# The order of routing work around the scores, in gated linear attention followed by a mixture of experts

## The chip, the cores and the metric

The kernel runs on one core of one Trainium2 chip. The metric is the device time of one launch in microseconds (us). A core has five engines, each with its own stream of instructions that it works through in order: TensorE (PE in the profile), VectorE (DVE), ScalarE (ACT), GpSimd (POOL) and SyncE (SP, which here issues transfers). An engine waits for another by semaphores. The kernel is scheduled by hand: on each engine, instructions stand in the order in which the program issues them, so moving a call in the program moves its instructions in their engines' streams.

## What is computed

Attention first: a recurrence over 768 steps for each of 4 x 8 heads of width 48. Its outputs, as 3072 rows of 384, go through a top-1 mixture of 8 experts.

```python
def _attn_ref(q, k, v, alpha):
    state = zeros(B, H, D, D)
    for t in range(S):                       # B, H, S, D = 4, 8, 768, 48
        state = alpha[:, :, t, :, None] * state + einsum('bhd,bhe->bhde', k[:, :, t], v[:, :, t])
        y[:, :, t] = einsum('bhd,bhde->bhe', q[:, :, t], state)

def _moe_ref(x, w_gate, w1, w2):             # x: 3072 x 384; E = 8; F = 1024
    logits = x @ w_gate
    expert_idx = argmax(logits, axis=1)
    probs = exp(logits - logits.max(-1)); probs /= probs.sum(-1) + 1e-9
    gate_w = probs[arange(N), expert_idx]
    # rows sorted by expert (stable), then for each expert e:
    #     y = relu(x_e @ w1[e]) @ w2[e],  put back in the rows' order
    return gate_w[:, None] * y
```

## The kernel before

The 3072 rows are 24 blocks of 128 (`NT` = 24), and the blocks go through a software pipeline two at a time ("a pair", s and s + 1). Block s is made in steps that lie in different pairs: `logs` and `cums` (decays), `operands` (k and q multiplied with decays, on GpSimd), `transposes`, `scores` (k with q, masked), `products` (k with v), `state`, `reads` and `weighs` (the output), `rows` (output as rows, and logits).

```python
def operands(s, k=nc.gpsimd, q=nc.gpsimd):       # L364, L366
    kq = kqb[s % 4]
    k.tensor_tensor(kq[:, 0, :, :D], d["k"][:], heads(d["icp"]), op=ALU.mult)
    q.tensor_tensor(kq[:, 1, :, :D], d["q"][:], d["cp"], op=ALU.mult)

def scores(s):                                   # L386 to L393
    sA = ps.tile([C, NP, C], F32, name="sA")     # one PSUM bank each
    sB = ps.tile([C, NP, C], F32, name="sB")
    ...                                          # products of kT and qT into sA and sB
    nc.vector.tensor_tensor(d["dA"][:], sA[:], cmask[...], op=ALU.mult)
    nc.scalar.copy(d["dB"][:], sB[:])
    nc.gpsimd.affine_select(d["dB"][:], d["dB"][:], ...)

def products(s):                                 # L452 to L460: into the same banks sA (s odd) or sB (s even)
    ...
    if s % 2:
        nc.vector.tensor_tensor(d["acc"][:], kv, st[s - 1]["U"][:, :, :D], op=ALU.add)   # accA
    else:
        nc.scalar.copy(d["acc"][:], kv)                                                  # accB

def rows(s):                                     # L478, L480
    ...                                          # products into xr
    nc.vector.reduce_sum(lgn[:, s, :], xr[...], axis=AX)       # logits, negated
```

The routing goes on beside attention. Four blocks are a group (the last two groups have two). When the logits of a group are there, `choose` finds each row's expert on VectorE and adds up on GpSimd how many rows before it have chosen each expert; later `rank_products` and `slots_of` make each row's slot of it, and `one_hots` prepares, for one block, what turns slots into lists of rows.

```python
def choose(g):                                   # g: the blocks of a group; L496 to L504
    nc.vector.tensor_reduce(lmin[:, t], lgn[:, t, :], axis=AX, op=ALU.min)
    nc.vector.tensor_tensor(sc[:], lgn[:, t, :], lmin[...], op=ALU.is_le)
    nc.vector.tensor_tensor(sc[:], sc[:], first_w[...], op=ALU.mult)
    nc.vector.reduce_max(top[:], sc[:], axis=AX)
    nc.vector.tensor_tensor(oh[:, t, :], sc[:], top[...], op=ALU.is_equal)
    for s in g:
        nc.gpsimd.tensor_add(ohs[:, s + 1, :], ohs[:, s, :], oh[:, s, :])

def one_hots(s, eng=nc.vector):                  # L579, L580
    nc.vector.tensor_scalar(oh_r[:, s, :], iota_r[:], scalar1=rc[:, 0, :], scalar2=None, op0=ALU.is_equal)
    eng.tensor_scalar(oh_c[:, s, :], iota_h[:], scalar1=rc[:, 1, :], scalar2=tokv[...], op0=ALU.is_equal, op1=ALU.mult)
```

The loop over pairs, cut to its order:

```python
for s in range(2, NT - 2, 2):
    ...
    reads(s); reads(s + 1)
    weighs(s, 0); weighs(s, 1)
    products(s + 1); products(s + 2)
    weighs(s + 1, 0); results_to(s, y, 0)        # yT, on VectorE
    weighs(s + 1, 1); results_to(s, y, 1)
    state(s + 1)
    if hots: one_hots(hots.pop(0))
    scores(s + 2)
    do(cums, s + 5)
    ranked = [rank_products(g, ...) for g in groups_of if g[-1] == s - 1]
    ...
    transposes(s + 3); do(operands, s + 5); state(s + 2)
    rows(s); keep_rows(s)
    do(cums, s + 6); do(transposes, s + 4)
    rows(s + 1); keep_rows(s + 1)
    scores(s + 3)
    do(operands, s + 6)
    store_rows(s)
    late_consts(s + 2); late_consts(s + 3)       # small constants, on GpSimd
    if s == ORD: choose(groups_of[-2])           # ORD = 20
    if hots: one_hots(hots.pop(0))
    for g in groups_of[:-2]:
        if g[-1] == s + 1: choose(g)             # s = 2, 6, 10, 14, 18
```

Behind the loop the last two blocks are finished, the lists of rows are made, and rows are gathered by them (`xg`). Meanwhile TensorE works ahead on expert 0's first layer, for the two blocks (EB = 2) of rows that were gathered early: 24 products of 128 x 128 by 128 x 256, `go_ahead(n)` issuing n of them. Then blocks 2 and 3 are turned (transposed by TensorE into `xtp`, copied by VectorE into `xT`) and the first layer goes on with their columns:

```python
go_ahead(9)
for k in range(EB, needed[0][-1] + 1):           # k = 2, 3
    turn_block(k)
    go_ahead(3)
go_ahead(99)
layer1(w_t[0][0], xT[0], h_t[0], EC, cols[0])
```

Of the kernel before, what the change touches and what calls it, by code (L numbers as in the profile page):

```python
# [18 lines left out]
def kernel(  # L19
# [70 lines left out]
    groups_of = [range(a, b) for a, b in zip(ends, ends[1:])]  # L90
    ORD = NT - 4
# [197 lines left out]
    with tc.tile_pool(name="ld", bufs=6) as ld, \  # L289
# [90 lines left out]
        def scores(s):  # L380
            d = st[s]
            sA = ps.tile([C, NP, C], F32, name="sA")
            sB = ps.tile([C, NP, C], F32, name="sB")
            for p in range(NP):
                for t, r in ((sA, 0), (sB, DP)):
                    nc.tensor.matmul(  # L386
                        t[:, p, :], lhsT=d["kT"][r : r + D, p, :], rhs=d["qT"][r : r + D, p, :], start=True, stop=True,
                    )
            d["dA"] = work.tile([C, NP, C], F32, name="dA")
            nc.vector.tensor_tensor(d["dA"][:], sA[:], cmask[:, None, :].to_broadcast([C, NP, C]), op=ALU.mult)  # L390
            d["dB"] = work.tile([C, NP, C], F32, name="dB")
            nc.scalar.copy(d["dB"][:], sB[:])  # L392
            nc.gpsimd.affine_select(  # L393
                d["dB"][:], d["dB"][:], compare_op=ALU.is_ge, fill=0.0,
                base=0, pattern=[[0, NP], [1, C]], channel_multiplier=-1,
            )
# [92 lines left out]
        def store_rows(s):  # L489
            r0 = s * C + (s >= NT // 2)  # L490
            nc.sync.dma_start(x_d[r0 : r0 + C, :], st[s]["xs"][:])

        def choose(g):

            t, n = slice(g[0], g[-1] + 1), len(g)
            nc.vector.tensor_reduce(lmin[:, t], lgn[:, t, :], axis=AX, op=ALU.min)  # L496
            sc = work.tile([C, n, E], F32, name="sc")
            nc.vector.tensor_tensor(sc[:], lgn[:, t, :], lmin[:, t].unsqueeze(2).to_broadcast([C, n, E]), op=ALU.is_le)
            nc.vector.tensor_tensor(sc[:], sc[:], first_w[:, None, :].to_broadcast([C, n, E]), op=ALU.mult)
            top = work.tile([C, n], F32, name="top")  # L500
            nc.vector.reduce_max(top[:], sc[:], axis=AX)
            nc.vector.tensor_tensor(oh[:, t, :], sc[:], top[:].unsqueeze(2).to_broadcast([C, n, E]), op=ALU.is_equal)
            for s in g:
                nc.gpsimd.tensor_add(ohs[:, s + 1, :], ohs[:, s, :], oh[:, s, :])  # L504

# [25 lines left out]
        def close_early(pos):  # L531

            cnt = work.tile([1, 1], F32, name="cnt")
            nc.vector.tensor_scalar(cnt[:], pos, scalar1=float(EC), scalar2=-1.0, op0=ALU.min, op1=ALU.mult)
            nc.vector.scalar_tensor_tensor(
                ohs[0:1, TE, 0:1], in0=cnt[:], scalar=float(EC), in1=ohs[0:1, TE, 0:1], op0=ALU.add, op1=ALU.add,
            )
# [47 lines left out]
        def tokens_of_slots(t0, t1):  # L585
            for t in range(t0, t1):
                nc.tensor.matmul(
                    route[:, :NC], lhsT=oh_r[:, t, :C], rhs=oh_c[:, t, :NC], start=(t == 0), stop=(t == NT - 1),
                    skip_group_check=True,
                )  # L590
# [16 lines left out]
        def do(f, i, *a):  # L607
            if 0 <= i < NT:
                f(i, *a)
# [17 lines left out]
        hots = []  # L627
# [72 lines left out]
        for s in range(2, NT - 2, 2):  # L700
            more_loads(2)
            if s == 2:
                store_rows(0)
            do(decay_out, s + 4)
            more_loads(2)

            for _ in range(8 if s > NT - 8 else 0):
                next(parts, None)
            y = results_of(s)
            reads(s)  # L710
            reads(s + 1)

            weighs(s, 0)
            weighs(s, 1)
            products(s + 1)
            products(s + 2)
            weighs(s + 1, 0)
            results_to(s, y, 0)
            weighs(s + 1, 1)
            results_to(s, y, 1)  # L720
            state(s + 1)
            do(logs, s + 5)
            if hots:
                one_hots(hots.pop(0))
            scores(s + 2)
            do(logs, s + 6)
            do(cums, s + 5)
            ranks = y[0][:].rearrange("r i p t -> r (i p t)")
            ranked = [rank_products(g, ranks[:, : len(g) * E]) for g in groups_of if g[-1] == s - 1]
            counts = ranks[:, C : C + E]  # L730
            if s in (TE, ORD):

                nc.tensor.matmul(
                    counts, lhsT=ones_sq[:], rhs=ohs[:, s, :], start=True, stop=True, skip_group_check=True,
                )
            if s == ORD:
                early_slots(ranks[:, 2 * C : 2 * C + EB * NQ])
                fetch_lot(0)
            for r in ranked if s < ORD else ():
                slots_of(*r)  # L740
            transposes(s + 3)
            do(operands, s + 5)
            state(s + 2)
            rows(s)
            keep_rows(s)
            store_rows(s - 1)
            if s == ORD:
                for r in ranked:
                    slots_of(*r)
                key = standing(counts[0:1, :])  # L750
                one_hots(hots.pop(0))
                one_hots(hots.pop(0))
                route = rps.tile([C, Dm], F32, name="cum")
                tokens_of_slots(0, TE)
            do(cums, s + 6)
            do(transposes, s + 4)
            more_loads(5)
            do(decay_in, s + 4)
            rows(s + 1)
            keep_rows(s + 1)  # L760
            if s == TE:
                close_early(counts[0:1, 0:1])
            scores(s + 3)
            do(operands, s + 6)
            store_rows(s)
            if s == 2:

                nc.sync.dma_start(x_d[N // 2 : N // 2 + 1, :], zero_w[:])
            late_consts(s + 2)
            late_consts(s + 3)  # L770
            if s == ORD:
                choose(groups_of[-2])
            if hots:
                one_hots(hots.pop(0))
            for g in groups_of[:-2]:
                if g[-1] == s + 1:
                    choose(g)
            for _ in range(4 if s == NT - 8 else 0):
                next(parts, None)
        for _ in parts:  # L780
# [19 lines left out]
        def go_ahead(n):  # L800
            for _ in range(n):
                next(ahead, None)


        s = NT - 2
# [26 lines left out]
        keep_rows(s + 1)  # L832
        store_rows(s + 1)
        choose(groups_of[-1])
        tokens_of_slots(TE, NT - 4)
        go_ahead(3)

# [204 lines left out]

    for i in range(E):
        if i == 0:
            go_ahead(9)
            for k in range(EB, needed[0][-1] + 1):
                turn_block(k)
                go_ahead(3)
# [3 lines that stand above are left out]
            if i == E - 1:  # L1052

                nc.gpsimd.drain()
            h_t[i] = (wk if i % 2 else early).tile([C, FB, CAP], F32, name="h_sb", bufs=1)
            if cols[i] < caps[i]:
                nc.gpsimd.memset(h_t[i][:, :, cols[i] : caps[i]], 0.0)
            layer1(w_t[i][0], xT[i], h_t[i], 0, cols[i])

        coming = list(needed[i + 1]) if i + 1 < E else []  # L1060
        for k in coming[:2]:
            turn_block(k)
        if i == 0:
            for n in (1, 2):
                weights1(n, True)
                weights2(n)
            gates_lot(0)
            gates_lot(1)
            for n in range(3, E):
                slots(n)  # L1070
            rows_out(o_idx[:], g_idx[:])
        if i + 3 < E:
            weights1(i + 3)
        for n, k in enumerate(ended[i]):
            if k not in gw:
                gates_lot([k in lot for lot in lots].index(True))
            results(k)
            if n == 0:
                for j in coming[2:]:
                    turn_block(j)  # L1080
                if i and i + 2 < E:

                    weights2(i + 2)
        if i in (0, 1, 3):
            fetch_lot((2, 3, None, 4)[i])
        if i == 0:
            nc.vector.tensor_copy(tot[:], route[0:1, NC : NC + E])
            extra_blocks()
# [48 lines left out]
```

## Time and profile before

| | us |
|---|---|
| time, median of three | 430.45 |
| lowest, highest | 429.62, 430.61 |
| span of the profiled execution | 427.8 |
| TensorE busy, 0 to 157.2 us of the span (attention, routing) | 153.16 |
| TensorE busy, 157.2 to 427.8 us (experts) | 265.62 |

The span runs from the first to the last instruction of one profiled execution. Timelines list a start, a length, the engine, the line of the kernel, the operation with its output and inputs, and in brackets how long the engine sat idle before it and what ended that. Matmuls are pipelined: each float32 product shows as two records, a record's length reaches over the start of the next, and what a stream of them costs is read from start to start.

### The profile page before, as it was taken

What the parts mean: (1) busy time and instruction counts of PE and PEld (TensorE: products, weight loads), DVE (VectorE), ACT (ScalarE), POOL (GpSimd) and SP (SyncE); (2) the same over time, 40 slices, a digit from 0 to 9 for tenths busy, and PEclk for the clock granted to TensorE, in tenths of its full rate; (3) what the DMA queues carried; (4) which work ended last, traced back from release to release, by engine and by line L of the source; (5) the groups of instructions that cost most, each with busy time, mean ns of one, the idle gap of its engine ahead of it and who ended that gap; (6) DMA issues with size and microseconds to landing.
All of it is one profiled execution on the core that took longest, in us unless ns stands there. A gap on an engine that the chain in (4) does not pass through costs nothing.

```text
span 427.8 us, 7702 instructions
## 1 busy us (share of the span) xinstructions
PE 418.8 (98%) x2990; PEld 284.2 (66%) x2990; DVE 142.4 (33%) x414; ACT 108.0 (25%) x230; POOL 141.5 (33%) x256
## 2 busy tenths in 40 slices
PE   8999999999999999999999999999999999999995
PEld 6888888888889887555645556655655455555452
DVE  6435667575858834711012101101201101111100
ACT  4465555555542321110111111011111110011011
POOL 4396776566665150160160120024010010011011
PEclk9999999999999999999999999999999999999998
DMA  8999999999877243994542710714620050000000
GB/s 170 175 171 215 192 201 205 204 199 194 176 192 218 77 114 102 395 397 159 180 124 69 248 47 3 277 68 114 224 108 18 2 184 20 0 33 20 1 33 30
DMA packets 132576, 59.43 MB, mean 139 GB/s; under 512 B 114614, under 2 KB 127452, under 8 KB 132538
## 3 DMA queue, kind: packets, MB, share of 16 engines
q1 hardware_dynamic: 127720, 48.96, 44.3%
q0 software_dynamic: 3328, 9.94, 7.2%
q8 instruction: 24, 0.39, 0.4%
q10 hardware_dynamic: 1490, 0.02, 0.2%
q14 instruction: 14, 0.11, 0.1%
HBM read 49.32 MB, written 9.98 MB: 139 GB/s over the span
## 4 chain that ended last, share of the span: by engine, by line
PE 60%; issue 28%; POOL 5%; DVE 4%; DMA 1%; ACT 1%; POOLq 0%; DVEq 0%
PE zp L988 16%; PE hp L972 14%; PE sA L386 5%; PE xr L478 5%; PE tp L373 5%; PE y L430 4%; PE cum L341 3%; POOL out_dram L994 3%; PE xr L616 2%; PE y L418 2%; PE xtp L964 1%; POOL xg L271 1%; PE hp L789 1%; PE sB L452 1%; DMA xg<-x_rows,g_idx 1%
## 5 line engine op out<-in xcount | busy, mean ns | idle before, releaser
L988 PE MATMUL zp<-w,h_sb 128*128 128x384 f32 (+2 forms) x560 | 137.1, 487 | 0.0
L972 PE MATMUL hp<-xT,w 128*128 128x416 f32 (+5 forms) x384 | 123.9, 482 | 0.0
L988 PEld LDWEIGHTS zp<-w,h_sb 128*128 128x128 f32 (+2 forms) x560 | 73.6, 163 | 56.4 <-issue 14.8
L972 PEld LDWEIGHTS hp<-xT,w 128*128 128x128 f32 x384 | 71.7, 190 | 50.7 <-issue 30.5
L994 POOL DMA_INDIRECT out_dram<-zo,o_idx x26 | 25.8, 992 | 213.4 <-ACT zo L993 208.4
L977 DVE TENSOR_SCALAR h_sb<-hp 128x416 f32<-128x416 f32 (+5 forms) x32 | 17.7, 554 | 148.1 <-PE hp L972 148.1
L993 ACT ACTIVATE zo<-zp,gw 128x384 f32<-128x384 f32 x26 | 15.1, 580 | 123.7 <-PE zp L988 119.1
L979 ACT ACTIVATE h_sb<-hp 128x416 f32<-128x416 f32 (+5 forms) x32 | 15.6, 487 | 106.1 <-PE hp L972 106.1
L386 PE MATMUL sA<-qT,kT 48*128 48x128 f32 x192 | 27.7, 284 | 1.4 <-DVE accA L458 1.2
L271 POOL DMA_INDIRECT xg<-x_rows,g_idx x26 | 25.1, 966 | 11.1 <-issue 6.4
L966 DVE COPY xT<-xtp 128x384 f32<-128x384 f32 (+3 forms) x29 | 13.1, 484 | 44.4 <-PE xtp L964 44.2
L386 PE MATMUL sB<-qT,kT 48*128 48x128 f32 x192 | 27.7, 285 | 0.0
L386 PEld LDWEIGHTS sA<-qT,kT 48*128 48x128 f32 x192 | 23.1, 187 | 6.0 <-issue 1.9
L373 PE MATMUL tp<-ident,kqb 128*128 128x128 f32 x192 | 25.6, 274 | 0.6 <-DVE qT L376 0.4
L364 POOL TENSOR_TENSOR kqb<-k_sb,icp 128x384 f32<-128x384 f32 x23 | 23.1, 1003 | 8.6 <-ACT icp L344 8.4
L430 PE MATMUL y<-dA,vb 128*64 128x128 f32 x192 | 25.9, 277 | 0.0
L373 PEld LDWEIGHTS tp<-ident,kqb 128*128 128x128 f32 x192 | 21.8, 141 | 6.0 <-issue 2.7
L430 PE MATMUL y<-dB,vb 128*64 128x128 f32 x192 | 25.4, 277 | 0.0
L478 PE MATMUL xr<-back,yT 128*128 128x104 f32 x192 | 25.2, 274 | 0.0
L478 PEld LDWEIGHTS xr<-back,yT 128*128 128x128 f32 x192 | 23.6, 192 | 1.0 <-ACT xs L485 0.4
L393 POOL TENSOR_SCALAR_AFFINE_SELECT dB<-dB 128x512 f32<-128x512 f32 x24 | 15.8, 658 | 22.6 <-ACT dB L392 20.5
L376 DVE COPY qT<-tp 128x512 f32<-128x512 f32 x24 | 16.6, 690 | 19.9 <-PE tp L373 19.7
(179 smaller groups left out, 446.8 us busy)
## 6 DMA issues: line engine op xcount, KB each, us to landing
w<-in_moe_w_dram SPq DMA_DIRECT2D x14, 1536.0 KB, 6.8
x_rows<-xs SPq DMA_DIRECT2D x24, 196.0 KB, 3.6
a_sb<-in_alpha_dram SPq DMA_DIRECT2D x24, 192.0 KB, 3.8
k_sb<-in_k_dram SPq DMA_DIRECT2D x24, 192.0 KB, 3.9
q_sb<-in_q_dram SPq DMA_DIRECT2D x24, 192.0 KB, 3.8
vb<-in_v_dram SPq DMA_DIRECT2D x24, 192.0 KB, 3.5
w<-in_moe_w_dram SPq DMA_DIRECT2D x12, 128.0 KB, 3.6
w<-in_moe_w_dram SPq DMA_DIRECT2D x8, 192.0 KB, 3.7
```

What stands on the lines that cost most here:

```text
L271: nc.gpsimd.indirect_dma_start(out=xg[:, j, :], out_offset=None, in_=x_d[: N + 1 if n else TE * C + 1, :], in_offset=bass.IndirectOffsetOn ...
L364: k.tensor_tensor(kq[:, 0, :, :D], d["k"][:], heads(d["icp"]), op=ALU.mult)
L373: nc.tensor.transpose(tp[:, p, :], pair(kqb[s % 4][:, i], p), ident[:])
L376: nc.vector.tensor_copy(d[n][:], tp[:])
L386: nc.tensor.matmul(t[:, p, :], lhsT=d["kT"][r : r + D, p, :], rhs=d["qT"][r : r + D, p, :], start=True, stop=True,)
L393: nc.gpsimd.affine_select(d["dB"][:], d["dB"][:], compare_op=ALU.is_ge, fill=0.0, base=0, pattern=[[0, NP], [1, C]], channel_multiplier=-1,)
L430: nc.tensor.matmul(d["y"][h][at(p, a) : at(p, a) + DP, n, :], lhsT=d["v"][:, 2 * p + a, :], rhs=d["d" + "AB"[a]][:, p, :], start=(first an ...
L478: nc.tensor.matmul(xr[:, p, :], lhsT=d["yT"][:, p // (NP // 2), p % (NP // 2), :], rhs=back[:, p, :], start=True, stop=True)
L972: nc.tensor.matmul(hp[:, c0:c1], lhsT=w1[:, a, f * C : (f + 1) * C], rhs=xT[:, a, c0:c1], start=(a == 0), stop=(a == DB - 1),)
L977: nc.vector.tensor_relu(h[:, f, c0:c1], hp[:, c0:c1])
L988: nc.tensor.matmul(zp[i * wd : (i + 1) * wd, :], lhsT=h[:, f, c : c + wd], rhs=w2[:, f, :], start=(f == 0), stop=(f == FB - 1), skip_group ...
L994: ins = nc.gpsimd.indirect_dma_start(out=out[:, :], out_offset=bass.IndirectOffsetOnAxis(ap=idx, axis=0), in_=zo[:], in_offset=None, bound ...
```

## The change

Three things are reordered; no work is added or taken away. First, `choose` is called ahead of the pair's last scores, `scores(s + 3)`, instead of at the end of the pair, so that VectorE works on it while TensorE still computes those scores; in pairs that choose nothing, a block's `one_hots` take that place. Second, GpSimd's adding up is split from `choose` into `sums`, and comes behind `operands(s + 6)`, so that the operands are not held up by a choice that isn't made yet. Third, at the start of expert 0, ten products go ahead of the first turn instead of nine, to give TensorE work while the gathered rows are on their way.

```diff
             nc.vector.tensor_tensor(oh[:, t, :], sc[:], top[:].unsqueeze(2).to_broadcast([C, n, E]), op=ALU.is_equal)
+
+        def sums(g):
             for s in g:
                 nc.gpsimd.tensor_add(ohs[:, s + 1, :], ohs[:, s, :], oh[:, s, :])
...
+            chosen = [g for g in groups_of[:-2] if g[-1] == s + 1] + ([groups_of[-2]] if s == ORD else [])
+            for g in chosen:
+                choose(g)
+            if hots and not chosen:
+                one_hots(hots.pop(0))
             scores(s + 3)
             do(operands, s + 6)
+            for g in chosen:
+                sums(g)
             store_rows(s)
...
             late_consts(s + 2)
             late_consts(s + 3)
-            if s == ORD:
-                choose(groups_of[-2])
-            if hots:
+            if hots and chosen:
                 one_hots(hots.pop(0))
-            for g in groups_of[:-2]:
-                if g[-1] == s + 1:
-                    choose(g)
...
         choose(groups_of[-1])
+        sums(groups_of[-1])
...
-            go_ahead(9)
+            go_ahead(10)
```

## The prediction

> **What bounds the kernel now.** I read the page's first part, which engine is busy, before anything else.
>
> ```profile
> PE 418.8 (98%) x2990; PEld 284.2 (66%) x2990; DVE 142.4 (33%) x414; ACT 108.0 (25%) x230; POOL 141.5 (33%) x256
> ```
>
> TensorE (PE) is busy for 418.8 of 427.8 us. The change takes no work off it, so all that can be won are holes in its stream. The time by windows says where they can be: the first 157.2 us (attention and routing) hold 153.16 us of busy PE, the other 270.6 us (experts) hold 265.62. The experts' part is untouched but for its first products, so the holes that matter lie before 157.2. Then the waits, for PE alone:
>
> ```profile
> PE sA L386 <- DVE accA L458: 1.2, 2, 0.7
> PE xtp L964 <- DMA xg<-x_rows,g_idx: 0.3, 1, 0.3
> ```
>
> (us in total, times, longest.) PE waits for VectorE (DVE) and for a gather. The ends of matmuls are modelled and overlap, so a wait read this way is too short. I measure a hole from start to start instead: in a pair of blocks with no hole the first score product starts 0.21 us after the last "weighs" product; any more is hole. PE's timeline at five places (start, length, what):
>
> ```profile
> 54.39 0.27 PE L430 MATMUL y<-dA,vb 128*64 128x128 f32 x1
> 54.60 0.37 PE L386 MATMUL sA<-qT,kT 48*128 48x128 f32 x1
> ...
> 65.44 0.27 PE L430 MATMUL y<-dA,vb 128*64 128x128 f32 x1
> 66.13 0.37 PE L386 MATMUL sA<-qT,kT 48*128 48x128 f32 x1 [0.41 <-DVE accA L458]
> ...
> 87.21 0.27 PE L430 MATMUL y<-dA,vb 128*64 128x128 f32 x1
> 88.23 0.37 PE L386 MATMUL sA<-qT,kT 48*128 48x128 f32 x1 [0.74 <-DVE accA L458]
> ...
> 114.32 0.60 PE L373 MATMUL tp<-ident,kqb 128*128 128x128 f32 x4
> 115.29 0.33 PE L373 MATMUL tp<-ident,kqb 128*128 128x128 f32 x1 [0.37 <-DVE qT L376]
> ```
>
> - 54.39 to 54.60 is the clean 0.21. 65.44 to 66.13 is 0.69: a hole of **0.48**. 87.21 to 88.23 is 1.02: a hole of **0.81**.
> - Four transposes take 4 x 0.11 = 0.44 elsewhere; here the fifth comes 0.97 after the first: a hole of **0.53**, and 0.1 more is lost as the stream refills (the first rows product follows 0.61 after it, for 4 x 0.11 and a little).
> - A fourth hole is small: the rank product starts 0.75 after the first of the two cumulative products at 67.22, but 1.00 after the one at 44.74: **0.25**.
>
> These four follow the pairs s = 6, 10, 14 and 2, just those at whose end `choose` runs on a full group while the operands are still being made. Why DVE is late is shown by its own timeline and GpSimd's (POOL) at the end of pair s = 10:
>
> ```profile
> 84.09 0.69 DVE L390 TENSOR_TENSOR dA<-sA,cmask 128x512 f32<-128x512 f32 x1 [0.89 <-PE sB L386]
> 85.69 0.81 DVE L498 TENSOR_TENSOR sc<-lgn,lmin 128x32 f32<-128x32 f32 x1
> 86.53 0.93 DVE L499 TENSOR_TENSOR sc<-sc,first_w 128x32 f32<-128x32 f32 x1
> 87.82 0.35 DVE L458 TENSOR_TENSOR accA<-sA,Ub 128x192 f32<-128x192 f32 x1
> ```
>
> POOL beside it:
>
> ```profile
> 85.45 1.00 POOL L364 TENSOR_TENSOR kqb<-k_sb,icp 128x384 f32<-128x384 f32 x1
> 86.41 1.00 POOL L366 TENSOR_TENSOR kqb<-q_sb,cpb 128x384 f32<-128x384 f32 x1
> ```
>
> The two `sc` operations handle 32 elements a row and take 0.81 and 0.93 us; each ends as one of POOL's operand products ends (86.45 and 87.41). In pair s = 18, where POOL has no operands left, the same two take 0.19 each. So `sc` is held up by POOL, `accA` waits behind it in DVE's order, and PE waits for `accA` to empty the bank `sA`. DVE sat idle for 0.89 us just ahead of `dA`, waiting for the scores.
>
> **What the Trainium skill says.** "SBUF — State Buffer", section "Who interferes with whom": a VectorE instruction with two SBUF inputs contends with a GpSimd instruction that reads SBUF, and so does one in a two-port mode, which `tensor_scalar` can enter; whoever is first keeps the shared ports for the whole instruction. The trace agrees: 0.19 against 0.81 to 0.93 for `sc`, and 0.34 against 0.66 to 0.79 for `oh_c`. The same section has one-SBUF-input instructions free of this; `dA` and `accA` read PSUM and one SBUF tensor, and they keep 0.67 to 0.69 and 0.35 throughout. "DMA: Bandwidth & Descriptors", section "Anatomy of one DMA", puts most of a DMA's fixed cost in the receipt of its write, so a gather's latency doesn't shrink here; the trace has 3.24 us from the issue of the first gather (151.01) to its use (landing at 154.25).
>
> **The change, part by part.** The build keeps each engine's instructions as they were in number; only their order changes, on DVE and POOL, and for one product on PE.
>
> 1. `choose` ahead of `scores(s+3)`. Its five operations now fall where DVE idles. Undisturbed, as at s = 18, they run from 129.69 to 130.76, so 1.07 us, after the last `lgn`. Idle time to fill is 0.89, so `dA` starts some 0.2 to 0.4 later. Does that hurt? At s = 6 `dA` ends at 62.57; the next product into `sA` starts at 63.74 and the first product that reads this `dA` only at 64.66: over 1.1 us of room. So nothing is paid.
> 2. What then stands ahead of `accA`: `dA`, and the two one-hots, which still meet POOL's select and first operand product. If each one-hot is held to the end of one POOL instruction, at s = 10 `oh_r` is free at 85.49 and `oh_c` at 86.45 to 86.75; `accA` ends at about 87.1, and PE wants its bank at 87.42 (87.21 + 0.21). That holds, by some 0.3. At s = 6 the same sum gives 64.9 against 65.65. So the holes of 0.48 and 0.81 close.
> 3. At s = 14 the chosen chain pushed `yT` to 110.38 while its products were done near 110.0, and then one-hots, `dA`, the slots and `qT` fell behind, each meeting POOL once more: `qT` started 4.6 us after the pair's first scores (109.96 to 114.56). In the next pair after s = 10 it was 3.65 (88.23 to 91.88) and no hole came of it. With `choose` gone from there, 3.65 is what I expect: 0.53 + 0.1 saved.
> 4. `sums` behind the operands, but now ahead of the late constants. At s = 2 POOL's eight constant operations (43.58 to 44.94) stood between operands and sums; the sums move from 44.94 to about 43.6 and the rank product no longer waits: 0.25 saved.
> 5. One-hots ahead of the scores in pairs that choose nothing: 0.6 us in an idle 0.89, at no cost and with no gain for PE, since those pairs have no hole.
> 6. Last loop pair, s = 20: `choose` (1.0 us) is put ahead of a `dA` that had no idle time ahead of it (started 138.76, ended 139.43). It will end near 140.5; the product that reads it starts at 140.50, and its partner waits for POOL's select until 140.67 in any case. 0 to 0.1 lost.
> 7. One product more ahead of the turn. The timeline there:
>
> ```profile
> 152.98 1.03 PE L789 MATMUL hp<-xT,w 128*128 128x256 f32 x4
> 154.30 0.55 PE L964 MATMUL xtp<-ident,xg 128*128 128x128 f32 x3 [0.30 <-DMA xg<-x_rows,g_idx]
> ...
> 156.31 1.03 PE L789 MATMUL hp<-xT,w 128*128 128x256 f32 x4
> 157.18 0.49 PE L972 MATMUL hp<-xT,w 128*128 128x192 f32 x2
> ```
>
> A product is two records of 0.216 (four start over 0.86), so 0.43. From the last record's slot, 152.98 + 0.86 = 153.84, to 154.30 is 0.46 of hole, into which 0.43 fit. But then one product, not two, stands after the second turn (156.31 to 156.75), and layer 1 needs the copy that ends at 156.87 (started 156.51, 0.36 long): it starts near 156.93 for 157.18. **0.25** saved.
>
> Sum: 0.48 + 0.81 + 0.63 + 0.25 + 0.25 = 2.42, less 0 to 0.1. From 430.45 that is **428.1**.
>
> **Rivals.**
> - *A new wait takes the place of the old one.* `oh_c`, still disturbed, might be held through both operand products, and `accA` at s = 10 come at 87.7 as before; or the later `dA` might stall the second "weighs". For it: the margin at s = 10 is 0.3. Against: each disturbed operation in the trace ended with the POOL instruction that it met first. It would leave 0.8 to 1.3 of the gain: about 429.3.
> - *The transfers become the bound.* In the windows between 29 and 107 us the mean busy share of the 16 DMA engines is 0.96 to 1.01. If they can't go faster, PE meets late loads and the time stays: 430.2. Against: the lead of the k loads, from issue to use, grows from 5.4 us (30.4 to 35.8) to 15 (92.9 to 108.0), with 3.9 to land; the loads outrun PE.
> - *Later `dA` in every choosing pair costs PE more than the late `accA` did.* Then 430.5 to 431.5. The 1.1 us of room speaks against it.
>
> **Range and chances.** The best case is all holes and the whole product: 430.45 - 2.6 = 427.8; the three runs before spread by 1.0, so I set the low end 0.8 below that, at 427.0. The high end, 429.6, has the first rival and half the spread. 2% would be 8.6 us; all holes of PE before 157.2 come to about 4, so neither outer chance is more than 0.01.
>
> **What would show it.** Right: `sc` at 0.19 in all groups, `accA` before 87, score products 0.21 after the last "weighs" product in every pair, the hole at the turn under 0.1. Wrong: PE waiting for `accA`, `dA` or the loads at the same places, or pairs that choose nothing getting longer.

## The result, and the profile after

| | before | changed |
|---|---|---|
| time, median of four (us) | 430.22 | 427.31 |
| lowest, highest | 429.62, 430.61 | 426.98, 427.69 |
| ratio, with its 95% interval | | 0.9934 (0.9917 to 0.9951) |
| span of the profiled execution | 427.8 | 425.9 |

The changed kernel is 0.66% faster: 2.9 us, and 2.1 to 3.6 by the interval. The places of the four holes, on TensorE's (PE's) timeline of the changed kernel; columns are start, length, engine, line, operation:

```profile
65.51 0.27 PE L430 MATMUL y<-dA,vb 128*64 128x128 f32 x1
65.71 0.37 PE L386 MATMUL sA<-qT,kT 48*128 48x128 f32 x1
...
86.80 0.27 PE L430 MATMUL y<-dA,vb 128*64 128x128 f32 x1
87.00 0.37 PE L386 MATMUL sA<-qT,kT 48*128 48x128 f32 x1
...
44.19 0.91 PE L341 MATMUL cum<-ln,cmask 128*128 128x384 f32 x2
44.94 0.18 PE L511 MATMUL y<-ohs,ones_sq 128*128 128x32 f16 x1
...
113.09 1.04 PE L373 MATMUL tp<-ident,kqb 128*128 128x128 f32 x8
113.97 0.26 PE L478 MATMUL xr<-back,yT 128*128 128x104 f32 x1
```

Twice 0.20 from the last "weighs" product to the first scores, where 0.69 and 1.02 stood; eight transposes in 0.88 without a break. The rank product of the first group starts 0.75 after its cumulative product (44.19 to 44.94), where it was 1.00. PE in the kernel before:

```profile
44.74 0.91 PE L341 MATMUL cum<-ln,cmask 128*128 128x384 f32 x2
45.74 0.18 PE L509 MATMUL y<-ohs,ones_sq 128*128 128x32 f16 x1
```

All four holes are closed. The reason shows on VectorE's (DVE's) timeline at the end of pair s = 10:

```profile
83.03 0.19 DVE L498 TENSOR_TENSOR sc<-lgn,lmin 128x32 f32<-128x32 f32 x1
83.26 0.19 DVE L499 TENSOR_TENSOR sc<-sc,first_w 128x32 f32<-128x32 f32 x1
...
84.42 0.74 DVE L581 TENSOR_SCALAR oh_r<-iota_r,rc 128x129 f16<-128x129 f32 x1
85.07 1.06 DVE L582 TENSOR_SCALAR oh_c<-iota_h,rc,tokv 128x129 f16<-128x129 f32 x1
86.05 0.34 DVE L458 TENSOR_TENSOR accA<-sA,Ub 128x192 f32<-128x192 f32 x1
```

The two `sc` now take 0.19 each, ahead of GpSimd's operands, which run from 85.04 to 87.01. It is the one-hots that meet GpSimd now (0.74 and 1.06, of some 0.3 each undisturbed), and yet `accA` ends at 86.39, 0.6 ahead of the scores that need its bank.

But PE has a new hole, of a kind that the prediction had only as a rival. PE, then ScalarE (ACT), then the load's issue (SPq), in pair s = 4 of the changed kernel:

```profile
46.33 0.61 PE L478 MATMUL xr<-back,yT 128*128 128x104 f32 x4
47.55 0.91 PE L341 MATMUL cum<-ln,cmask 128*128 128x384 f32 x2 [0.61 <-ACT cpb L345]
```
ScalarE's instruction ahead of it:
```profile
46.21 0.52 ACT L330 ACTIVATE ln<-a_sb 128x384 f32<-128x384 f32 x1 [1.29 <-DMA a_sb<-in_alpha_dram]
```
and the transfer that it waits for:
```profile
41.63 0.58 SPq L309 DMA_DIRECT2D a_sb<-in_alpha_dram  x1
```

The load of alpha is issued at 41.63 and used at 46.21, ScalarE idle for 1.29 us; its decays come late, and the cumulative product starts 1.22 after the rows products instead of some 0.45: a hole of 0.77. In the profile of before the same load already held ScalarE up, but PE didn't feel it. ScalarE, then the load's issue, in the kernel before:

```profile
45.93 0.52 ACT L330 ACTIVATE ln<-a_sb 128x384 f32<-128x384 f32 x1 [0.46 <-DMA a_sb<-in_alpha_dram]
...
42.04 0.58 SPq L309 DMA_DIRECT2D a_sb<-in_alpha_dram  x1
```

Counted from the loop's first product (29.20 before, 28.65 after), ScalarE could use the load 0.83 us later than before, and PE came to its cumulative product 0.24 sooner. So most of this hole is a later load, and the smaller part PE's lead.

### The profile page after: what moved, and what is told of

Same layout as the page of the kernel before. It is cut to its first block, busy times and chain, and to the rows that moved or that the text cites. A ratio compares the mean times of both kernels' runs of the same rounds, so it can differ in the third digit from the quotient of the medians.

```text
span 425.9 us, 7698 instructions
## 1 busy us (share of the span) xinstructions
PE 418.0 (98%) x2990; PEld 283.5 (67%) x2990; DVE 138.3 (32%) x414; ACT 108.0 (25%) x230; POOL 141.0 (33%) x256
## 4 chain that ended last, share of the span: by engine, by line
PE 61%; issue 28%; POOL 5%; SPq 2%; DMA 2%; ACT 1%; POOLq 0%; DVE 0%; ACTq 0%
PE zp L994 16%; PE hp L978 14%; PE sA L386 5%; PE y L430 5%; PE xr L478 4%; PE tp L373 4%; PE cum L341 3%; POOL out_dram L1000 3%; PE y L418 2%; PE hp L794 2%; PE xr L618 2%; PE xtp L970 1%; POOL xg L271 1%; PE sB L452 1%; DMA a_sb<-in_alpha_dram 1%
## 5 line engine op out<-in xcount | busy, mean ns | idle before, releaser
L386 PEld LDWEIGHTS sB<-qT,kT 48*128 48x128 f32 x192 | 23.1, 187 | 0.0
```

What stands on the lines that cost most here:

```text
L386: nc.tensor.matmul(t[:, p, :], lhsT=d["kT"][r : r + D, p, :], rhs=d["qT"][r : r + D, p, :], start=True, stop=True,)
```

## Experiments

The part ahead of the loop is the same code in all runs here, but its length differs between executions: the loop's first product comes at 28.65 to 29.97 us. So profiles are compared by pieces: from the loop's first product to the issue of the first gather behind the loop ("loop"), from there to expert 0's layer 1 ("turn"), and from there to the last product, which is 265.6 to 265.9 in every run. "Late load" is the hole of the second cumulative product in pair s = 4.

| run | median us | ratio to before (95%) | loop | turn | late load |
|---|---|---|---|---|---|
| before | 430.2 | | 121.81 | 6.16 | 0 |
| changed | 427.31 | 0.9917 to 0.9951 | 120.33 | 6.16 | 0.77 |
| changed, again | 427.85 | 0.9929 to 0.9955 | 120.69 | 5.92 | 1.14 |
| choice and sums alone | 427.84 | 0.9931 to 0.9957 | 119.49 | 6.14 | 0 |
| tenth product alone | 430.02 | 0.9989 to 1.0005 | 121.83 | 6.10 | 0 |
| operands first, choice late | 427.68 | 0.9926 to 0.9962 | 119.84 | 6.22 | 0.28 |
| late choice, sums ahead of constants | 431.71 | 1.0021 to 1.0049 | 124.06 | 6.01 | 0.84 |
| changed, one-hots back | 427.64 | 0.9925 to 0.9957 | 119.63 | 5.98 | 0 |
| changed, sums beside the choice | 428.55 | 0.9951 to 0.9978 | 120.20 | 6.29 | 0 |
| changed, alpha sooner | 428.20 | 0.9946 to 0.9971 | 119.89 | 6.16 | 0 |
| changed, stores later | 428.91 | 0.9941 to 0.9972 | 120.58 | 6.01 | 0 |
| changed, slots behind qT | 427.48 | 0.9920 to 0.9951 | 120.66 | 5.99 | 1.10 |
| alpha sooner, slots behind qT | 427.28 | 0.9924 to 0.9952 | 119.53 | 5.92 | 0 |
| stores later, slots behind qT | 427.31 | 0.9918 to 0.9946 | 119.35 | 5.92 | 0 |

**The changed kernel once more.** No edit.

> The changed kernel as it is, once more. Closed holes alone would save 0.25 + 0.48 + 0.81 + 0.63 = 2.2 us, and in the first profile the turn added nothing. If the wait of the cumulative product for late decays (a hole of 0.77 us at 47.55 us) is a property of the changed order, it comes again in this profile, and the gain is near 1.5 to 2; if it is chance of that one execution, it is gone here and the gain is 2.2 to 3.

Measured: 427.85 (ratio 0.9942), the four holes closed, the late load back with 1.14 us. So it isn't chance of one execution; the next runs show that it isn't in every one either. The theory to be tested from here: the choice's `sc` was held by GpSimd's operands, and nothing else of the change counts.

**The two parts apart.**

```diff
# choice and sums alone
-            go_ahead(10)
+            go_ahead(9)
# tenth product alone: the kernel before, with
-            go_ahead(9)
+            go_ahead(10)
```

> Choice ahead of the scores and sums behind the operands, but nine products ahead of the turn as before. If the tenth product is worth 0.25 us as predicted, this saves 0.25 less than the changed kernel; if the second gather's landing sets layer 1, as the changed profile suggests, it saves the same within 0.1: 2.2 to 2.9 us under before, with the hole of 0.46 ahead of the first turn back and none at layer 1's start.

> The kernel before with ten products ahead of the turn. Predicted step: 0.25 us saved. Rival: 0.0 saved, layer 1 starting within 0.1 us of 157.2 less whatever the head of the execution shifts, since the second turn waits for its gather and layer 1 for its copy. The four holes of before (0.25, 0.48, 0.81, 0.53) stay.

Measured: the choice alone has the whole gain (0.9944), with a loop of 119.49, 2.32 under before's 121.81. The tenth product alone saves 0.2 at the median, its interval holds 1, and the four holes are all there. The changed kernel's turn shows where it went:

```profile
152.24 0.51 PE L970 MATMUL xtp<-ident,xg 128*128 128x128 f32 x3
152.59 1.46 PE L794 MATMUL hp<-xT,w 128*128 128x256 f32 x6
154.06 0.55 PE L970 MATMUL xtp<-ident,xg 128*128 128x128 f32 x3
154.44 0.60 PE L794 MATMUL hp<-xT,w 128*128 128x256 f32 x2
155.14 0.73 PE L978 MATMUL hp<-xT,w 128*128 128x192 f32 x3
```

The hole ahead of the first turn is filled. But the six records from 152.59 take 1.30 from start to start, so the second turn could start at 153.89, and starts at 154.06, behind its own gather; and layer 1 starts 0.27 late, behind the copy of that turn. From the first gather's issue (148.98) to layer 1 it is 6.16, as before. In the run with the tenth product alone it is the first gather that comes late: its turn starts 3.39 after the issue, where the others with ten products have 3.26 to 3.28.

**Operands first, the choice left late.**

```diff
+            chooses = any(g[-1] == s + 1 for g in groups_of[:-2])
+            if chooses:
+                do(operands, s + 6)
             scores(s + 3)
-            do(operands, s + 6)
+            if not chooses:
+                do(operands, s + 6)
```

> The kernel before, with the choice late as it was, but in the pairs that choose GpSimd makes the operands ahead of the masking of the last scores, so that it is done with them sooner. If the holes at s = 6 and 10 come from VectorE's two-input operations (sc) being held by GpSimd's operand products, sc falls from 0.8 to 0.9 us to 0.2 to 0.6 us and these holes shrink by at least 0.5 us each, without the choice having been moved: 0.8 to 1.8 us under before. If they come from the choice's place in VectorE's order alone, sc keeps its length, the holes stay, and the time is before's within 0.3 or worse by the later mask.

Measured: 0.9944, as much as by moving the choice. VectorE at the end of pair s = 10 in this run:

```profile
85.03 0.82 DVE L579 TENSOR_SCALAR oh_r<-iota_r,rc 128x129 f16<-128x129 f32 x1
85.76 0.67 DVE L580 TENSOR_SCALAR oh_c<-iota_h,rc,tokv 128x129 f16<-128x129 f32 x1
86.34 0.17 DVE L496 TENSOR_REDUCE lmin<-lgn 128x4 f32<-128x32 f32 x1
86.55 0.19 DVE L498 TENSOR_TENSOR sc<-lgn,lmin 128x32 f32<-128x32 f32 x1
86.78 0.19 DVE L499 TENSOR_TENSOR sc<-sc,first_w 128x32 f32<-128x32 f32 x1
```
GpSimd in the same stretch:
```profile
84.75 1.01 POOL L366 TENSOR_TENSOR kqb<-q_sb,cpb 128x384 f32<-128x384 f32 x1
85.71 0.63 POOL L393 TENSOR_SCALAR_AFFINE_SELECT dB<-dB 128x512 f32<-128x512 f32 x1
```

VectorE's instructions and their order are before's; only GpSimd is done by 86.34, and `sc` takes 0.19. The holes at s = 6, 10 and 14 are gone. So it was the meeting of the two engines, and not the choice's place in VectorE's stream as such. The rank product's hole is gone too, although the sums still stand behind the constants: GpSimd no longer sits idle for 1.34 us ahead of the mask, and comes to its sums 1.28 us sooner, counted from the loop's first product. So that hole had a second remedy beside moving the sums.

**Sums ahead of the constants, the choice left late.**

```diff
             scores(s + 3)
             do(operands, s + 6)
+            if s == ORD: choose(groups_of[-2]); sums(groups_of[-2])
+            if hots: one_hots(hots.pop(0))
+            for g in groups_of[:-2]:
+                if g[-1] == s + 1: choose(g); sums(g)
             store_rows(s)
             late_consts(s + 2)
             late_consts(s + 3)
-            ...                                  # the same calls, without sums
```

> The kernel before, with the choice still behind the scores and the operands, but it and its sums ahead of GpSimd's late constants. VectorE's order is before's. Expected: the rank product's hole of 0.25 us near 45.7 us closes, the holes of 0.48, 0.81 and 0.53 stay; 0 to 0.3 us saved. If the split of the sums were what matters, the gain would be above 1 us.

Measured: 1.6 us slower at the median, which I had not expected. The rank product's hole does close. The three others stay (the one after s = 6 with 0.37), and two new ones of 0.56 (and 0.17 of refilling) come in the pairs after s = 6 and 10: GpSimd now waits for the late choice and does its constants behind it, when VectorE makes its next one-hots and slots. There `rc_i` takes 0.83 and `rc` 0.85, each ending as an operand product ends, and qT is late. Of the 2.25 us that the loop is longer in this profile, these two places are 1.46, and 0.84 is the late load.

**Sums back beside the choice, in the changed kernel.**

```diff
             for g in chosen:
                 choose(g)
+                sums(g)
...
-            for g in chosen:
-                sums(g)
```

> The changed kernel, with the sums put back beside the choice, so ahead of GpSimd's mask of the scores and of the operands. The choice ends just before that mask can start, so if GpSimd's order hardly matters the mask and the operands come up to 0.7 us later and nothing waits for them: the changed kernel's time within 0.3. If the split is needed, TensorE waits for the masked scores or for the operands by 0.3 to 1 us in each of five pairs: 1 to 3 us over the changed kernel.

Measured: 428.55, which is 0.7 over the choice alone, and the loop is 0.7 longer too. In the last pair the sums hold up GpSimd's mask, which starts at 138.53 behind them; PE starts nothing for 0.38 until 139.21, and the stretch from its scores to the next rank product is 0.34 longer than in the changed kernel (3.76 for 3.42). Another 0.26 at 58.3 is not due to the sums: there ScalarE waits 0.69 for a load of alpha. So what the profile shows the split to be worth is about 0.3, in one pair, and not the 1 to 3 of the rival.

**One-hots back behind the scores.**

```diff
-            if hots and not chosen:
-                one_hots(hots.pop(0))
             scores(s + 3)
...
-            if hots and chosen:
+            if hots:
```

> The changed kernel, with the one-hots of pairs that choose nothing back behind the scores. The prediction has no gain from having moved them: the time is the changed kernel's within 0.3. If they did help, it is 0.5 us or more over it, with holes of TensorE in the pairs that choose nothing.

Measured: 0.9941, as the changed kernel; no hole in any pair. This part of the change does nothing for the time.

**The late load: alpha sooner, stores later.**

```diff
# alpha sooner
-                (("a", 1), ...) if x == 7 else (("k", 0), ("v", -2), ("a", 1), ("q", 0))
+                (("a", 1), ...) if x == 7 else (("k", 0), ("a", 1), ("v", -2), ("q", 0))
-            if s == 2:                           # store of the row of zeros
+            if s == 10:
# stores later
-            xs = work.tile([C, W], F32, name="xs", bufs=3)
+            xs = work.tile([C, W], F32, name="xs", bufs=7)
-            store_rows(s - 1)                    # and store_rows(0), store_rows(s) alike
+            held.append(s - 1)
+            give_back(s, 1 if s < 12 else 2)     # stores so many of those held, from s = 6 on
```

> The changed kernel with the load of alpha issued ahead of that of v in each round of loads, and the row of zeros stored at s = 10 and not at s = 2. If the hole of 0.77 at 47.55 us comes from transfers issued too late, alpha is issued some 0.7 us sooner, the hole is gone, and the time is 0.5 to 0.8 us under the changed kernel's. If the hole is chance, or sits with the DMA engines' load rather than with the issue, the time is the same within 0.3.

> The changed kernel, with the stores of the first five blocks of rows held back until pair s = 6 and given out again one or two at a time (seven buffers in place of three). If the new hole near 47.5 us is for the transfers' own pace early on, five stores of 196 KB less leave the loads of alpha about a microsecond sooner there: no hole, and 0.4 to 1.0 us under the changed kernel. If the hole comes from something else, the time stays within 0.3.

Measured: in both the late load's hole is gone, and both are no faster than the changed kernel, but at the median 0.3 and 1.1 over its second measurement (the intervals overlap). With the decays in time, the operands come in time too, and meet the slots. PE and VectorE in pair s = 4, stores later:

```profile
49.90 0.77 PE L373 MATMUL tp<-ident,kqb 128*128 128x128 f32 x5 [1.00 <-DVE qT L376]
```
VectorE ahead of it:
```profile
47.24 1.05 DVE L524 TENSOR_SCALAR rc_i<-slot_i 128x4 int32<-128x4 int32 x1
48.33 0.92 DVE L528 CAST rc<-rc_i 128x8 f32<-128x8 int32 x1
49.17 0.68 DVE L376 COPY qT<-tp 128x512 f32<-128x512 f32 x1
```

Two operations on 4 and 8 elements a row take 1.05 and 0.92 us, while GpSimd's operand products run from 47.28 to 49.22; in the changed kernel, whose operands came later, they took 0.16 and 0.17. qT is late by that much: a hole of 1.17 (0.35 with alpha sooner). It is a close meeting: in the choice alone, with no late load either, `rc` was done at 46.65, 0.1 after an operand product began at 46.55, and took 0.17.

**Slots behind qT.**

```diff
-            for r in ranked if s < ORD else ():
-                slots_of(*r)
             transposes(s + 3)
             ...
             rows(s); keep_rows(s); store_rows(s - 1)
+            for r in ranked:
+                slots_of(*r)
             if s == ORD:
-                for r in ranked: slots_of(*r)
                 ...
```

> The changed kernel, with the five operations of the slots behind the copy of qT and the sums of the logits, so in VectorE's idle time of about 1 us ahead of the pair's second copy of qT. In the changed kernel's own profiles qT was not late, so by itself this saves 0 to 0.5 us; the wait for late decays near 47.5 us stays where loads are late. If the slots' place doesn't matter, no difference beyond 0.3.

> Both: alpha's loads sooner and the slots behind qT. If the sooner loads were given back only because the slots then met GpSimd's operands and made qT late (a hole of 0.35), that hole goes and none comes: 0.5 to 1 us under the changed kernel. If another wait follows, the time is the changed kernel's within 0.3.

> Both: the first stores held back and the slots behind qT. The hole of 1.17 (qT late behind the slots) should go: 1.0 us under the run with the stores held back alone, so 0 to 0.5 us under the changed kernel. If the hole is not from the slots' operations meeting the operands, it stays.

Measured: alone it changes nothing (427.48, and the late load is there with 1.10). On top of either mend of the loads it takes 0.9 and 1.6 us off at the median (0.36 and 1.23 off the loops of the profiles), and no hole is left in the loop. At 427.28 and 427.31 these two can't be told from the changed kernel's 427.31 and 427.85; what they have over it is at most the late load, which comes only in some executions (with over 0.7 us in four of the ten profiles here whose loads and stores are ordered as in before, and in none of the other four). In those four ScalarE can use the load 17.56 to 17.93 us after the loop's first product, in the six others 16.57 to 17.07, and in the four with sooner loads 16.17 to 16.48. One of the four late ones is the run of the late choice with sums ahead, so a late load doesn't need the choice's new place. What shifts the load from one execution to the next stays open.

## Why the prediction was right

427.31 lies in the range, 0.8 under the point. Step by step:

1. *The choice in idle time, `dA` later by 0.2 to 0.4.* Right, and it is only 0.13: `dA` starts 1.22 after `lgn` at s = 10 (82.59 to 83.81), for 1.09 before. No product waits for it.
2. *One-hots each held to the end of one GpSimd instruction, `accA` ahead of its need by some 0.3.* Right: both are held, and the margin is 0.6. Holes of 0.48 and 0.81 closed.
3. *The hole at s = 14.* Right: 0.53 and the refilling of 0.17 (I had 0.1) are gone.
4. *0.25 at the first rank product.* Closed, but not always kept: where alpha's load is late, PE comes to that wait 0.25 sooner, and waits 0.25 longer. This is what was true of the rival of the transfers. I had judged it by how the leads of the k loads grow over the whole stage; but PE waits for one load, and alpha's in pair s = 4 had a lead of only 3.9 us before (42.04 to 45.93), with ScalarE already waiting for it; another had 3.5 (52.84 to 56.31).
5. *One-hots, no gain.* Right.
6. *Last pair, 0 to 0.1 lost.* Right: no difference shows there.
7. *Tenth product, 0.25.* Over-sized. 0.24 came where the second turn wasn't late (turn 5.92), 0 in the first profile (6.16), about 0.1 on average over the table (6.13 with nine products, 6.05 with ten), which is less than such profiles differ (5.92 to 6.29). I took the starts of the turns as given by PE's stream, but each also waits for its gather, which the tenth product can't hasten.

The sum of the holes, 2.17, is in the profiles: the loop shrinks by 2.32 where no load is late (121.81 to 119.49). The times, 2.9 and then 2.3 us less than before's, agree with that within their intervals. That they lie so near the forecast of 2.35 is in part luck: the tenth product gave less than I counted, and the late load, which I had not counted, took 0.77 and 1.14 in the two profiles. That GpSimd's operands were the cause of the three larger holes is shown by the run that moved them and not the choice.

## What to carry to other kernels

Where one engine is busy all the time, a wait of the others is worth just the hole that it makes there; measure it from start to start. Where a tiny operation takes several times as long as elsewhere in the same trace, see whether it ends with a long instruction of another engine, as `sc` did here. Moving either of the two was worth the same here; but look for the next tiny operation that slides into the same place. Before closing a hole, look what else lies within its length behind it, such as a load with a short lead.

## What was new about the hardware

The one-hots and the slots' cast are held just as two-input operations are: in the profile of before, `rc` (8 elements a row) took 0.17 at 46.70, with no operand product beside it, and 0.92 at 68.95, beside one that ran from 68.83 to 69.83. The Trainium skill ("SBUF — State Buffer", section "Who interferes with whom") names copies, casts and `tensor_scalar` among those that can contend with GpSimd; here they cost as much as `sc`. And the same code ahead of the loop took 28.65 to 29.97 us: the first warm-up products come 0.426 apart, later 0.216, and when that turns differs between executions (after 5.26 us in before's profile, 3.97 in the changed kernel's). These 1.3 us are about half of what the change gains, so profiles of single executions are compared by pieces.
